# One stretch of row-group products in the output stage, and a later second spatial tile, in a fused attention and gMLP kernel

## The chip, the cores and the metric

The kernel runs on one core of a Trainium2 chip. The metric is device time in microseconds (us) for one execution; the median of several runs is compared. The core has five engines that matter here, each with its own in-order instruction stream: TensorE (PE in the profile; its weight loads are PEld), VectorE (DVE), ScalarE (ACT), GpSimd (POOL) and SyncE (SP). SP does no arithmetic; it issues transfers, as ACT and POOL can too. Transfers issued by one engine leave in the order of its stream. Sums of products land in PSUM, a small memory of banks with 512 float32 per partition each, and have to be read out before a bank is written for something else.

## The reference

Input x is [2048, 512] in bfloat16. The output is x plus two branches of the normalised x:

```python
xn = layernorm(x)                       # over the 512 features, eps 1e-5, no weights
# branch A: 32 heads of 16; each position attends to 8 earlier ones, 2 apart
q, k, v = xn @ wqkv                     # 512 -> 3 * 512
logits = (q[s] . k[s - 2 * w]) / 4      # w = 0..7, masked before position 0
a = softmax(logits over w) @ v[s - 2 * w] @ wo
# branch B: gated MLP with a mixing over positions
z = gelu(xn @ w_in)                     # 512 -> 2 * 688
z1, z2 = z[:, :688], layernorm(z[:, 688:])
g = w_sp @ z2 + b_sp[:, None]           # [2048, 2048] @ [2048, 688]
out = x + a + (z1 * g) @ w_out          # 688 -> 512
```

## The kernel before, in words

The 2048 positions are 16 tiles of 128 rows. The first third of the kernel normalises x, transposes it (`xnT`) and makes z2 (`z`, `h`), q and k (`k`) and z1 (`y`). ACT takes the gelu of each z2 tile and with it a row sum (`zsum`), then squares the tile to get a row sum of squares (`zsq`).

**Statistics of z2.** `z2_stats` (lines 246 to 252) runs once for four tiles (steps `zs0`, `zs4`, `zs8`, `zs12`): three small DVE operations make the mean and the variance, GpSimd adds EPS (line 251) and raises to the power -1/2 (line 252). Then DVE normalises the four tiles (`zn`, line 258). Between the two, DVE's list has larger work: the products of q with shifted k (line 307, steps `m` and `j`), whose folds (`f`, `p`, and transfers `d`) lead to the logits.

**The middle.** TensorE runs, in this order, the spatial tiles `M0` and `M1` (line 390: 32 products each, for 128 output positions), the head sums `S00` to `S13` (line 321, which turn the folded products into logits) mixed with eight `v` pairs (line 286), and then `M2` to `M15`. Each spatial tile fills one of three PSUM pairs, is emptied by ACT with its bias into one of three buffers (line 393), and is multiplied by z1 in a gate `g` on DVE (line 398). SP then transposes the gated rows by a transfer (line 400). The spatial weights come in eight pieces `W0` to `W7` (line 383), each for two spatial tiles, in three buffers; the buffer of `W3` is that of `W0`, so `W3` waits for `M1`.

**Softmax and attention on DVE.** For either half `th` of the positions: the maximum and its subtraction (`x`), an exponential on ACT (`e`), the sum (`u`), its inverse on ACT (`i`), the scaling (`c`), then twelve steps `a`: eight products of v with a weight (line 363), three additions (line 367), and a last addition (line 376) that writes the attention result for TensorE. All steps but the first of each half (w = 0) read v shifted by up to 14 rows, so they need the halo of v, two small transfers issued by GpSimd in `H` (lines 292 and 293), which in turn need all v copies of ACT.

**The output stage.** The 16 tiles form four groups of four (`groups`): two for the first half of the positions, two for the second. An output tile is the sum of five products with all 128 rows (`gated_full`, line 429), two with 32 and 16 rows for the remaining 48 gated features (`gated_rest`, line 444), and 16 with 32 rows for attention (`attention_out`, line 457). The products with 32 rows or fewer run for four tiles at once, each in its own group of 32 rows of the array ("row groups"). For the remainders, SP or GpSimd first copies rows to the right partitions (`spread_rest`, line 452). Eight banks hold two groups. `finish` and `finish_pair` add x (lines 462 and 469) and send the tile out.

**What sets the order.** Two lists are written by hand, `ten` (TensorE and ACT) and `vec` (DVE, with the transfers that belong to its steps). `advance` walks them: it takes steps in list order, and ahead of a step whatever `needs` names from the other list. The engines' streams follow that order. Waits between engines are added from what an instruction reads and writes.

Of the kernel before, what the change touches and what calls it, by code (L numbers as in the profile page):

```python
# [8 lines left out]
F32 = mybir.dt.float32  # L9
# [4 lines left out]
P = 128  # L14
# [24 lines left out]
def kernel(  # L39
# [36 lines left out]
    zmean = sb.tile([P, NT], F32, name="zmean")  # L76
    zvar = sb.tile([P, NT], F32, name="zvar")
    zrstd = sb.tile([P, NT], F32, name="zrstd")
    zbias = sb.tile([P, NT], F32, name="zbias")
    b16 = sb.tile([NT, P], BF16, name="b16")  # L80
    b_col = sb.tile([P, NT], F32, name="b_col")
    stmp = sb.tile([P, 4, GS], F32, name="stmp")
# [156 lines left out]

    def z2_square(i):  # L240

        A.activation(z2_junk[:], z2[:, i, :], ACT.Square, accum_out=zsq[:, i:i + 1])  # L242

    z2_junk = sb.tile([P, FH], BF16, name="z2_junk")

    def z2_stats(i, n):
        s = slice(i, i + n)
        V.tensor_scalar(zmean[:, s], zsum[:, s], 1.0 / FH, None, ALU.mult)
        V.tensor_tensor(zvar[:, s], zmean[:, s], zmean[:, s], ALU.mult)
        V.scalar_tensor_tensor(zvar[:, s], zsq[:, s], 1.0 / FH, zvar[:, s], ALU.mult, ALU.subtract)  # L250
        G.tensor_scalar(zvar[:, s], zvar[:, s], EPS, 1.0, ALU.add, ALU.mult)
        G.tensor_tensor(zrstd[:, s], zvar[:, s], mhalf[:, 0:n], ALU.pow)

    def z2_norm(i, on_act):
        if on_act:
            A.activation(z2[:, i, :], z2[:, i, :], ACT.Identity, bias=zbias[:, i:i + 1], scale=zrstd[:, i:i + 1])
        else:
            V.tensor_scalar(z2[:, i, :], z2[:, i, :], zmean[:, i:i + 1], zrstd[:, i:i + 1],
                            ALU.subtract, ALU.mult)

    def z1_tile(i):
        pz = z_part(i, 0)
# [176 lines left out]
    def gated_rest(tiles, start, last=None):  # L439
        for x in range(2):  # L440
            for i in tiles:
                rows, u, w = rest_of(i, x)
                for b, c in last if last and i == tiles[3] else [(po[i], slice(0, D))]:
                    PE.matmul(b[:, c], u, w[:, c], start=(start and x == 0), stop=False, tile_position=(rows.start, 0))  # L444

    def spread_rest(th, g):
        t = slice(2 * g * P, 2 * (g + 1) * P)
# [6 lines left out]
    def attention_out(th, s, pos, start, stop):  # L454
        for d in range(DH):
            for g in range(4):
                PE.matmul(pos[g], op[32 * g:32 * g + 32, th, d, s * P:(s + 1) * P], wo_r[32 * g:32 * g + 32, d, :],  # L457
                          start=(start and d == 0), stop=(stop and d == DH - 1), tile_position=(32 * g, 0))

    def finish(i, po, cols=slice(0, D), q=SP):  # L460
        o = nxt("ot", ot)
        V.tensor_tensor(o[:, cols], po[:, cols], xr[i // 8][:, i % 8, cols], ALU.add)  # L462
        q.dma_start(out2[i * P:(i + 1) * P, cols], o[:, cols])

    def finish_pair(i):

# [10 lines left out]
    for i in range(5, NT):  # L477
# [2 lines left out]
    vec = front.split() + """  # L480
        zs0 LW m00 zn0 zn1 zn2 zn3 j00 f00 p00 K m01 d01 m02 d02 zs4 m03 d03 zn4 zn5 zn6 zn7
        p01 p02 zs8 m10 d10 zn8 zn9 zn10 zn11 p03 W1 zs12 m11 zn12 zn13 zn14 zn15 f11 p11 p10 m12 d12
        m13 f13 x0 p13 p12 W2 W3 g0 u0 g1 c0 x1 a0.0 u1 g2
        c1 g3 a0.1 a0.2 a0.3 g4 a0.4 g5 a0.5 a0.6 a0.7 g6 a0.8 g7 a0.9 g8 a0.10 g9 a0.11 g10
        a1.0 a1.1 g11 a1.2 a1.3 g12 a1.4 g13 X1 a1.5 g14 a1.6 a1.7 g15 a1.8 a1.9 F0 a1.10 a1.11 F1 F2
    """.split()
    ten = """
        T0 B T1 GL BC z0 z1 h0 T3 h1 z2 h2 z3 h3 LZ k00 k01 q0 k02 q1 k03 q2 z4 h4 z5 q3 h5 k10 k12 k11 k13
        W0 q4 k20 z6 h6 q5 k21 z7 h7 q6 k22 z8 h8 q7 k23 z9 h9 q8 k30 z10 h10 q9 k31 z11 h11 q10
        k32 z12 h12 q11 k33 z13 h13 z14 h14 q12 z15 h15 y0 y1 q13 y2 y3 q14 y4 y5 q15 y6 y7 y8 y9 y10 y11 y12 y13 y14 y15  # L490
        EL M0 M1 S00 S01 v0 S02 S03 v1 S10 S11 v2 v3 e0 v4 v5 i0 v6 S13 S12 v7 H
        e1 M2 i1 M3 M4 O4 M5 W4 W5 M6 O0 M7 W6 M8 O1 M9 W7 M10 O2 M11 O3 M12 X0 M13 M14 M15 Q0 Q2 Q3
    """.split()

    def needs(n):
# [36 lines left out]
            return ["xeui"["euic".index(k)] + a]  # L532
        if k == "a":

            return ["c" + a[0]] + ([] if a == "0.0" else ["H"]) + ([f"y{x}" for x in range(NT)] if a[2:] == "11" else [])
        if k == "H":
            return [f"v{x}" for x in range(8)] + ["d12"]
        if k == "M":
# [9 lines left out]
        if k == "O":  # L548
            return [f"y{x}" for x in range(NT)] + ["H"]
        if k == "Q":  # L550
            return [["a0.11", "g7", "O4"], ["g7"], ["a1.11", "g15", "F0"], ["F2"]][i]
        if k == "F":
            return [f"Q{[0, 0, 2][i]}", f"X{i // 2}"]
        if k == "X":
            return ["M11" if i == 0 else "M13"]
        return []


    banks = [mm[1][:, 0, :], mm[1][:, 1, :], mm[2][:, 0, :], mm[2][:, 1, :],
             mm[0][:, 0, :], aux[0][:], mm[0][:, 1, :], aux[1][:]]  # L560
    groups = [[8 * th + 2 * g + t for g in range(4)] for th in range(2) for t in range(2)]
    po = {i: banks[4 * (n % 2) + g] for n, tiles in enumerate(groups) for g, i in enumerate(tiles)}

    def out_pair():

        first, second = groups[0], groups[1]
        for i in first:
            gated_full(i, po[i], True, False)
        gated_rest(first, False)
        gated_rest(second, True)  # L570
        attention_out(0, 0, [po[i] for i in first], False, True)
        attention_out(0, 1, [po[i] for i in second], False, False)
        for i in second:
            gated_full(i, po[i], False, True)

    def out_group(n):
        tiles = groups[n]
        for i in tiles:
            gated_full(i, po[i], True, False)
        gated_rest(tiles, False)  # L580
        attention_out(n // 2, n % 2, [po[i] for i in tiles], False, True)

    def out_last(n):

        tiles = groups[n]
        th, s, last = n // 2, n % 2, tiles[-1]
        hb = [po[last], po[groups[n - 1][0]]]
        cols = [slice(0, D // 2), slice(D // 2, D)]
        for d in range(DH):
            for g in range(4):  # L590
                a = slice(32 * g, 32 * g + 32)
                for dd, b, c in [(d, po[tiles[g]], slice(0, D))] if g < 3 else \
                        [(2 * d % DH + x, hb[d // 8], cols[d // 8]) for x in range(2)]:
                    PE.matmul(b[:, c], op[a, th, dd, s * P:(s + 1) * P], wo_r[a, dd, c],  # L594
                              start=(dd == 0), stop=False, tile_position=(32 * g, 0))
        gated_rest(tiles, False, list(zip(hb, cols)))
        for i in tiles[:3]:
            gated_full(i, po[i], False, True)
            finish(i, po[i])
        for b, c, q in zip(hb, cols, (SP, A)):  # L600
            gated_full(last, b, False, True, c)
            finish(last, b, c, q)

    gates, done = {}, set()
    at = [attend(0), attend(1)]
# [1 line left out]
    def do(n):  # L607
# [9 lines left out]
        elif n[:2] == "zs":  # L617
            z2_stats(int(n[2:]), 4)
        elif n[:2] == "zn":
            z2_norm(int(n[2:]), False)  # L620
        elif n == "z0":
            gates["z0"], gates["z1"] = nxt("mm", mm), nxt("mm", mm)
            for t, hh in ((0, 0), (0, 1), (1, 0)):
# [28 lines left out]
        elif k == "W":  # L652
            load_wsp(i)
        elif k == "O":
            load_wo(i) if i < 4 else load_wout()
        elif k == "X":
            load_res(i)
        elif n == "GL":
            A.preload_act_table(ACT.Gelu_apprx_tanh)
        elif n[:2] == "EG":  # L660
            A.preload_act_table(ACT.Gelu_apprx_tanh)
        elif n[:2] == "EL":
            A.preload_act_table_set("natural_log_exp_and_others")
        elif k == "Q":
            [out_pair, None, lambda: out_group(2), lambda: out_last(3)][i]()
        elif k == "F":
            tiles = groups[i]
            for t in (0, 2):
                if (i, t) in ((0, 0), (0, 2), (1, 0)):
                    finish_pair(tiles[t])  # L670
                else:
                    finish(tiles[t], po[tiles[t]])
                    finish(tiles[t + 1], po[tiles[t + 1]])
        elif k == "e":
            softmax_exp(i)
        elif k == "i":
            softmax_inv(i)
        elif k == "s":
            ln_stats(i)
        elif k == "R":  # L680
            ln_root_act(i, 1)
        elif k == "V":
            ln_inv(i)
        elif n == "LE":
            load_early()
        elif k == "r":
            ln_root(i, 1)
        elif k == "n":
            ln_norm(i)
        elif k == "t":  # L690
            turn_dma(i)
        elif n == "LZ":
            load_x(12, 4, A)
        elif n == "LX":
            load_tokens()
        elif n == "LW":
            load_weights()
        elif k == "m":
            run(prod_ops(th, w2)[0])
        elif k == "j":  # L700
            run(prod_ops(th, w2)[1])
        elif k == "f":
            prod_ops(th, w2)[2]()
        elif k == "p":
            prod_ops(th, w2)[3]()
        elif k == "d":
            fold_dma(th, w2)
        elif k == "K":
            k_halo()
        elif k == "x":  # L710
            run(softmax_max(i))
        elif k == "u":
            run(softmax_sum(i))
        elif k == "c":
            run(softmax_scale(i))
        elif k == "g":
            gate(i, gates[i])
            if i in (7, 9, 11, 13, 15):
                for g in range(4) if i == 7 else [(i - 9) // 2]:
                    spread_rest(i // 8, g)  # L720
        elif k == "a":
            at[int(a[0])][int(a[2:])]()
# [54 lines left out]
```

## Time and profile before

| what | us |
|---|---|
| median of 3 runs | 200.67 (200.47 to 200.71) |
| profiled execution, its own time | 200.75 |
| its span | 199.0 |
| TensorE busy | 194.4 |
| DVE busy | 176.0 |
| ACT busy | 89.2 |
| GpSimd busy | 46.7 |
| spatial products (line 390) | 75.0 |
| attention products and additions on DVE (lines 363 and 367) | 36.0 and 26.5 |

Times in the profile count from the start of the span. A timeline line has the start, the time, the engine, the line of the kernel, the operation and what it writes and reads; lines of the same kind that follow each other are merged (x4 is four of them), and a bracket gives the idle time of the engine ahead of the first and what ended it. TensorE's products overlap, so the time of one (0.38 for 512 columns) is longer than the distance of two (0.216).

The stages by TensorE's rows: z2, q, k and z1 until 72; `M0`, `M1` until 81.7; head sums and v pairs until 97.3; `M2` to `M15` until 162.7; the output stage until 196.1; then the last addition and transfer.

### The profile page before, as it was taken

What the parts mean: (1) busy time and instruction counts of PE and PEld (TensorE: products, weight loads), DVE (VectorE), ACT (ScalarE), POOL (GpSimd) and SP (SyncE); (2) the same over time, 40 slices, a digit from 0 to 9 for tenths busy, and PEclk for the clock granted to TensorE, in tenths of its full rate; (3) what the DMA queues carried; (4) which work ended last, traced back from release to release, by engine and by line L of the source; (5) the groups of instructions that cost most, each with busy time, mean ns of one, the idle gap of its engine ahead of it and who ended that gap; (6) DMA issues with size and microseconds to landing.
All of it is one profiled execution on the core that took longest, in us unless ns stands there. A gap on an engine that the chain in (4) does not pass through costs nothing.

```text
span 199.0 us, 3879 instructions
## 1 busy us (share of the span) xinstructions
PE 194.4 (98%) x1597; PEld 119.5 (60%) x1604; DVE 176.0 (88%) x193; ACT 89.2 (45%) x145; POOL 46.7 (23%) x71
## 2 busy tenths in 40 slices
PE   7999999999999999999999999999999999999993
PEld 2655555555666666666666666666666664444662
DVE  4899789999889899997898999999999999997233
ACT  3869779899888671489753111111222110000000
POOL 4277540139496701200060000101010000000000
PEclk9999999999999999999999999999999999999999
DMA  5999679399637961904999979999998934632033
GB/s 179 340 186 179 133 176 291 87 203 204 133 79 135 156 136 32 182 3 74 199 191 145 238 190 257 114 262 180 236 191 106 215 82 120 183 109 90 19 105 105
DMA packets 64610, 31.09 MB, mean 156 GB/s; under 512 B 53456, under 2 KB 62800, under 8 KB 64464
## 3 DMA queue, kind: packets, MB, share of 16 engines
q1 hardware_dynamic: 59136, 19.24, 48.5%
q0 software_dynamic: 2192, 6.75, 17.6%
q10 hardware_dynamic: 3264, 4.86, 10.4%
q8 instruction: 12, 0.20, 0.4%
q14 instruction: 6, 0.05, 0.1%
HBM read 10.13 MB, written 2.10 MB: 61 GB/s over the span
## 4 chain that ended last, share of the span: by engine, by line
PE 98%; issue 0%; DVE 0%
PE mm L390 38%; PE mm L226 19%; PE mm L271 14%; PE mm L286 7%; PE mm L429 7%; PE mm L457 5%; PE mm L405 2%; PE aux L429 2%; PE mm L594 1%; PE mm L444 1%; PE aux L321 1%; PE aux L212 1%; PE aux L594 0%; DVE z L462 0%; PE mm L645 0%
## 5 line engine op out<-in xcount | busy, mean ns | idle before, releaser
L390 PE MATMUL mm<-z,wsp 128*128 128x344 bf16 x512 | 75.0, 309 | 0.0
L390 PEld LDWEIGHTS <-wsp 128*128 128x128 bf16 x512 | 50.0, 98 | 24.9 <-issue 0.4
L226 PE MATMUL mm<-wts,xnT 128*128 128x344 bf16 x256 | 39.3, 309 | 0.1
L393 ACT ACTIVATE qk<-mm,b_col 128x688 bf16<-128x688 f32 x16 | 13.3, 833 | 52.6 <-PE mm L390 52.6
L363 DVE TENSOR_TENSOR prod<-vp,a_sb 128x4096 bf16<-128x4096 bf16 x16 | 36.0, 2281 | 0.0
L307 DVE TENSOR_TENSOR prod<-qk 128x4096 bf16<-128x4096 bf16 (+1 forms) x16 | 31.6, 2019 | 1.5 <-ACT qk L273 1.5
L226 PEld LDWEIGHTS <-xnT 128*128 128x128 bf16 x256 | 24.8, 98 | 13.3 <-DMA xnT<-z 0.3
L271 PE MATMUL mm<-xnT,wts 128*128 128x512 bf16 x124 | 28.7, 379 | 0.2
L367 DVE TENSOR_TENSOR prod<-prod,prod 128x8192 bf16<-128x8192 bf16 x6 | 26.5, 4418 | 0.1
L271 PEld LDWEIGHTS <-wts 128*128 128x128 bf16 x128 | 14.5, 114 | 12.2 <-DMA xnT<-z 0.4
L273 ACT CAST qk<-mm 128x1024 bf16<-128x1024 f32 x16 | 16.2, 1012 | 5.0 <-PE mm L271 4.1
L429 PE MATMUL mm<-wts,qk 128*128 128x512 bf16 (+1 forms) x62 | 14.2, 370 | 0.4 <-issue 0.3
L286 PE MATMUL mm<-xnT,wts 128*32 128x512 bf16 x256 | 14.5, 379 | 0.0
L263 ACT ACTIVATE z<-mm 128x688 bf16<-128x688 f32 x16 | 11.9, 742 | 4.4 <-PE mm L226 4.4
L429 PEld LDWEIGHTS <-qk 128*128 128x128 bf16 x85 | 8.2, 98 | 9.2 <-issue 0.6
L452 POOL DMA_DIRECT2D qk<-qk x6 | 3.0, 500 | 42.3 <-DMA qk<-z 42.3
L237 ACT ACTIVATE z<-mm 128x688 bf16<-128x688 f32 x16 | 11.9, 744 | 2.0 <-PE mm L226 1.9
L190 DVE BATCH_NORM_STATS2 stats<-z 128x6 f32<-128x512 bf16 x16 | 11.0, 685 | 1.8 <-DMA z<-in_A_x_dram 1.8
L316 POOL DMA_DIRECT2D prod<-prod x8 | 7.3, 994 | 22.3 <-DVE prod L307 22.3
L242 ACT ACTIVATE z_junk<-z 128x688 bf16<-128x688 bf16 x16 | 12.3, 772 | 0.0
L286 PEld LDWEIGHTS <-wts 128*32 128x32 bf16 x256 | 9.5, 138 | 4.3
L462 DVE TENSOR_TENSOR z<-mm,wsp 128x512 bf16<-128x512 f32 (+1 forms) x8 | 5.0, 651 | 7.8 <-PE mm L457 4.7
(98 smaller groups left out, 195.1 us busy)
## 6 DMA issues: line engine op xcount, KB each, us to landing
prod<-prod POOLq DMA_DIRECT2D x8, 512.0 KB, 5.2
wts<-in_A_wo_dram ACTq DMA_DIRECT2D x4, 512.0 KB, 5.6
out_dram<-z SPq DMA_DIRECT2D x9, 128.0 KB, 1.7
z<-in_A_x_dram SPq DMA_DIRECT2D x4, 256.0 KB, 4.3
wts<-in_A_wqkv_dram SPq DMA_DIRECT2D x2, 512.0 KB, 5.1
wsp<-wsp POOLq DMA_DIRECT2D x2, 512.0 KB, 5.7
wsp<-in_A_x_dram ACTq DMA_DIRECT2D x1, 1024.0 KB, 5.7
wsp<-in_A_x_dram SPq DMA_DIRECT2D x1, 1024.0 KB, 6.3
```

Source lines behind the costliest of these rows:

```text
L226: PE.matmul(pz[:, hh, 0:FHALF], xnT[:, kc, i * P:(i + 1) * P], w_z2[:, hh, kc] if part else w_z1[:, kc, hh * FHALF:(hh + 1) * FHALF], star ...
L237: A.activation(z2[:, i, :].rearrange("p (a b) -> p a b", a=2), pz[:, :, 0:FHALF], ACT.Gelu_apprx_tanh, accum_out=zsum[:, i:i + 1])
L242: A.activation(z2_junk[:], z2[:, i, :], ACT.Square, accum_out=zsq[:, i:i + 1])
L271: PE.matmul(pq[:, cc, :], w_c[:, kc], xnT[:, kc, t0:t0 + D], start=(kc == 0), stop=(kc == C - 1))
L273: A.copy(qk[b // 2][:, a, 2 * c2:2 * c2 + 2, o:o + D], pq[:])
L286: PE.matmul(pv[32 * g:32 * g + 32, dd, :], w, r, start=(kc == 0), stop=(kc == C - 1), tile_position=(0, 32 * g))
L307: ops.append(lambda ww=ww, k=k, c=c: V.tensor_tensor(pr[:, ww, c], q[:, c], k[:, c], ALU.mult))
L363: return lambda: V.tensor_tensor(dst, vp[:, :, th, off:off + GS], a_sb[:, th, w].unsqueeze(1).broadcast_to([P, DH, GS]), ALU.mult)
L367: return lambda: V.tensor_tensor(dst, dst, x, ALU.add)
L390: PE.matmul(pg[:, hh, 0:FHALF], w[:, k, (j % 2) * P:(j % 2 + 1) * P], z2[:, k, hh * FHALF:(hh + 1) * FHALF], start=(k == 0), stop=(k == NT ...
L393: A.activation(g.rearrange("p (a b) -> p a b", a=2), pg[:, :, 0:FHALF], ACT.Identity, bias=b_col[:, j:j + 1])
L429: PE.matmul(po[:, cols], uT[th][:, m, t0:t0 + P], wout[:, m, cols], start=(start and m == 0), stop=(stop and m == MF - 1))
```

## The change

It has four parts.

1. ACT's square of z2 is scaled by 688 to the power -1/2, so that its sum is already the mean of squares; the third DVE operation adds EPS and subtracts the squared mean; GpSimd is left with the power alone. (An unused variant of the normalisation goes too.)
2. `M1` moves on TensorE from behind `M0` to behind the last v pair and the halo `H`.
3. DVE's list is reordered from `W2` on: gates come later or earlier by a few steps, `W3` comes behind `g1`, the first attention step needs only the v pairs and no halo, and the first finished group (`F0`) moves behind the last attention step.
4. The output stage runs the whole products of both first groups, then the row-group products of all four groups, then the whole products of the last two groups. The remainders of group 2 wait for `F0`, which empties their banks. For the very last tile, DVE adds x to what its bank holds (`sofar`) ahead of its whole products; these then go in two column halves into two banks, and are added to `sofar`.

```diff
-        A.activation(z2_junk[:], z2[:, i, :], ACT.Square, accum_out=zsq[:, i:i + 1])
+        A.activation(z2_junk[:], z2[:, i, :], ACT.Square, scale=float(FH) ** -0.5, accum_out=zsq[:, i:i + 1])
...
-        V.scalar_tensor_tensor(zvar[:, s], zsq[:, s], 1.0 / FH, zvar[:, s], ALU.mult, ALU.subtract)
-        G.tensor_scalar(zvar[:, s], zvar[:, s], EPS, 1.0, ALU.add, ALU.mult)
+        V.scalar_tensor_tensor(zvar[:, s], zsq[:, s], EPS, zvar[:, s], ALU.add, ALU.subtract)
         G.tensor_tensor(zrstd[:, s], zvar[:, s], mhalf[:, 0:n], ALU.pow)
...
-        m13 f13 x0 p13 p12 W2 W3 g0 u0 g1 c0 x1 a0.0 u1 g2
-        c1 g3 a0.1 a0.2 a0.3 g4 a0.4 g5 a0.5 a0.6 a0.7 g6 a0.8 g7 a0.9 g8 a0.10 g9 a0.11 g10
-        a1.0 a1.1 g11 a1.2 a1.3 g12 a1.4 g13 X1 a1.5 g14 a1.6 a1.7 g15 a1.8 a1.9 F0 a1.10 a1.11 F1 F2
+        m13 f13 x0 p13 p12 W2 u0 g0 c0 x1 a0.0 u1 a0.1 g1 W3 c1 a0.2 g2 a0.3 g3
+        a0.4 g4 a0.5 g5 a0.6 a0.7 g6 a0.8 g7 a0.9 a0.10 g8 a0.11 g9
+        a1.0 a1.1 g10 a1.2 a1.3 g11 a1.4 g12 X1 a1.5 a1.6 g13 a1.7 g14 a1.8 g15 a1.9 a1.10 a1.11 F0 F1
...
-        EL M0 M1 S00 S01 v0 S02 S03 v1 S10 S11 v2 v3 e0 v4 v5 i0 v6 S13 S12 v7 H
-        e1 M2 i1 M3 M4 O4 M5 W4 W5 M6 O0 M7 W6 M8 O1 M9 W7 M10 O2 M11 O3 M12 X0 M13 M14 M15 Q0 Q2 Q3
+        EL M0 S00 S01 v0 S02 S03 v1 S10 S11 v2 v3 e0 v4 v5 i0 v6 S13 S12 v7 H
+        M1 e1 M2 i1 M3 M4 O4 M5 W4 W5 M6 O0 M7 W6 M8 O1 M9 W7 M10 O2 M11 O3 M12 X0 M13 M14 M15 Q0 Q2 Q3 Q4
...
-            return ["c" + a[0]] + ([] if a == "0.0" else ["H"]) + ([f"y{x}" for x in range(NT)] if a[2:] == "11" else [])
+            return ["c" + a[0]] + ([f"v{x}" for x in range(8)] if a == "0.0" else ["H"]) + ([f"y{x}" for x in range(NT)] if a[2:] == "11" else [])
...
-            return [["a0.11", "g7", "O4"], ["g7"], ["a1.11", "g15", "F0"], ["F2"]][i]
+            return [["a0.11", "g7", "O4"], [], ["a1.11", "g15", "F0"], ["F1"], ["Q3"]][i]
...
-    banks = [mm[1][:, 0, :], mm[1][:, 1, :], mm[2][:, 0, :], mm[2][:, 1, :],
+    banks = [mm[1][:, 0, :], mm[2][:, 0, :], mm[1][:, 1, :], mm[2][:, 1, :],
              mm[0][:, 0, :], aux[0][:], mm[0][:, 1, :], aux[1][:]]
...
+    def out_first():
+
+        for i in groups[0] + groups[1]:
             gated_full(i, po[i], True, False)
+        for n in (0, 1):
+            gated_rest(groups[n], False)
+        for n in (0, 1):
+            attention_out(0, n, groups[n], groups[n])
+
+    def out_tiled(n):
+        gated_rest(groups[n], True)
+        attention_out(1, n - 2, groups[n], [last])
+
+    def out_last():
+        V.tensor_tensor(sofar, po[last], xr[1][:, last % 8, :], ALU.add)
+        for i in groups[2] + groups[3][:3]:
             gated_full(i, po[i], False, True)
+            finish(i)
+
+        for b, c, q in ((po[last], slice(0, D // 2), SP), (po[groups[2][0]], slice(D // 2, D), A)):
+            gated_full(last, b, True, True, c)
+            o = nxt("ot", ot)
+            V.tensor_tensor(o[:, c], b[:, c], sofar[:, c], ALU.add)
+            q.dma_start(out2[last * P:(last + 1) * P, c], o[:, c])
```

More of the change, by code (lines that the diff above doesn't have):

```diff
@@ L78 @@
     zrstd = sb.tile([P, NT], F32, name="zrstd")
-    zbias = sb.tile([P, NT], F32, name="zbias")
     b16 = sb.tile([NT, P], BF16, name="b16")
@@ L249, in z2_stats, with z2_norm @@
         V.tensor_tensor(zvar[:, s], zmean[:, s], zmean[:, s], ALU.mult)
-        V.scalar_tensor_tensor(zvar[:, s], zsq[:, s], 1.0 / FH, zvar[:, s], ALU.mult, ALU.subtract)
-        G.tensor_scalar(zvar[:, s], zvar[:, s], EPS, 1.0, ALU.add, ALU.mult)
+        V.scalar_tensor_tensor(zvar[:, s], zsq[:, s], EPS, zvar[:, s], ALU.add, ALU.subtract)
         G.tensor_tensor(zrstd[:, s], zvar[:, s], mhalf[:, 0:n], ALU.pow)
[L254 to L259, printed above, removed]
+    def z2_norm(i):
+        V.tensor_scalar(z2[:, i, :], z2[:, i, :], zmean[:, i:i + 1], zrstd[:, i:i + 1], ALU.subtract, ALU.mult)
     def z1_tile(i):
@@ L437, in rest_of, with gated_rest @@
         return rows, uB[i // 8][rows, t0:t0 + P], wB[rows]
-    def gated_rest(tiles, start, last=None):
+    def gated_rest(tiles, start):
         for x in range(2):
@@ L442, in gated_rest @@
                 rows, u, w = rest_of(i, x)
-                for b, c in last if last and i == tiles[3] else [(po[i], slice(0, D))]:
-                    PE.matmul(b[:, c], u, w[:, c], start=(start and x == 0), stop=False, tile_position=(rows.start, 0))
+                PE.matmul(po[i], u, w, start=(start and x == 0), stop=False, tile_position=(rows.start, 0))
     def spread_rest(th, g):
@@ L452, in spread_rest, with attention_out, finish @@
                 (SP if th else G).dma_start(dst[32 * g:32 * g + n, t], uT[th][r:r + n, MF, t])
-    def attention_out(th, s, pos, start, stop):
+    def attention_out(th, s, tiles, stop):
         for d in range(DH):
             for g in range(4):
-                PE.matmul(pos[g], op[32 * g:32 * g + 32, th, d, s * P:(s + 1) * P], wo_r[32 * g:32 * g + 32, d, :],
-                          start=(start and d == 0), stop=(stop and d == DH - 1), tile_position=(32 * g, 0))
-    def finish(i, po, cols=slice(0, D), q=SP):
+                PE.matmul(po[tiles[g]], op[32 * g:32 * g + 32, th, d, s * P:(s + 1) * P], wo_r[32 * g:32 * g + 32, d, :],
+                          start=False, stop=(tiles[g] in stop and d == DH - 1), tile_position=(32 * g, 0))
+    def finish(i):
         o = nxt("ot", ot)
-        V.tensor_tensor(o[:, cols], po[:, cols], xr[i // 8][:, i % 8, cols], ALU.add)
-        q.dma_start(out2[i * P:(i + 1) * P, cols], o[:, cols])
+        V.tensor_tensor(o, po[i], xr[i // 8][:, i % 8, :], ALU.add)
+        SP.dma_start(out2[i * P:(i + 1) * P, :], o)
     def finish_pair(i):
@@ L550, in needs @@
         if k == "Q":
-            return [["a0.11", "g7", "O4"], ["g7"], ["a1.11", "g15", "F0"], ["F2"]][i]
+            return [["a0.11", "g7", "O4"], [], ["a1.11", "g15", "F0"], ["F1"], ["Q3"]][i]
         if k == "F":
-            return [f"Q{[0, 0, 2][i]}", f"X{i // 2}"]
+            return ["Q0", "X0"]
         if k == "X":
@@ L562 @@
     po = {i: banks[4 * (n % 2) + g] for n, tiles in enumerate(groups) for g, i in enumerate(tiles)}
-    def out_pair():
-        first, second = groups[0], groups[1]
-        for i in first:
+    last = groups[3][3]
+    sofar = wsp_r[1].bitcast(F32)[:, 0:D]
+    def out_first():
+        for i in groups[0] + groups[1]:
             gated_full(i, po[i], True, False)
[L569 to L573, printed above, removed]
-            gated_full(i, po[i], False, True)
@@ L576, in out_group @@
[L576 to L602, printed above, removed]
+        for n in (0, 1):
+            gated_rest(groups[n], False)
@@ L619, in do @@
         elif n[:2] == "zn":
-            z2_norm(int(n[2:]), False)
+            z2_norm(int(n[2:]))
         elif n == "z0":
@@ L664, in do @@
         elif k == "Q":
-            [out_pair, None, lambda: out_group(2), lambda: out_last(3)][i]()
+            [out_first, None, lambda: out_tiled(2), lambda: out_tiled(3), out_last][i]()
         elif k == "F":
-            tiles = groups[i]
             for t in (0, 2):
-                if (i, t) in ((0, 0), (0, 2), (1, 0)):
-                    finish_pair(tiles[t])
-                else:
-                    finish(tiles[t], po[tiles[t]])
-                    finish(tiles[t + 1], po[tiles[t + 1]])
+                if (i, t) == (1, 2):
+                    finish(groups[i][2])
+                    finish(groups[i][3])
+                else:
+                    finish_pair(groups[i][t])
         elif k == "e":
```

## The prediction

> **What bounds the kernel now.** I read the page first (busy shares, then the chain that ended last), then the list of waits, then the timeline around the three places that the change touches.
>
> ```profile
> PE 194.4 (98%) x1597; PEld 119.5 (60%) x1604; DVE 176.0 (88%) x193; ACT 89.2 (45%) x145; POOL 46.7 (23%) x71
> ...
> PE 98%; issue 0%; DVE 0%
> ```
>
> The reader is to see that TensorE is busy for 98% of the span and that the chain never leaves it. An edit therefore gains only if it takes work or gaps off TensorE, and loses exactly as much as it makes TensorE wait. DVE, with 88%, has the least room behind it. The profiled execution took 200.75 us (span 199.0), 0.08 above the median of the runs, 200.67; the sum below is made against 200.75 and 0.08 is taken off at the end.
>
> **Part 1, z2's statistics.** Of each of the four groups, the GpSimd addition of EPS (line 251) goes; EPS and the scale move into operations that are there already, at the same price. The timeline around the third group:
>
> ```profile
> 54.49 0.16 DVE L250 SCALAR_TENSOR_TENSOR zvar<-zsq,zvar 128x4 f32<-128x4 f32 x1
> 54.57 4.49 DVE L307 TENSOR_TENSOR prod<-qk 128x4096 bf16<-128x4096 bf16 x2
> 54.74 2.16 POOL L251 TENSOR_SCALAR zvar<-zvar 128x4 f32<-128x4 f32 x1 [2.68 <-DVE zvar L250]
> 56.99 2.96 POOL L252 TENSOR_TENSOR zrstd<-zvar,mhalf 128x4 f32<-128x4 f32 x1
> ...
> 59.99 0.46 DVE L258 TENSOR_SCALAR z<-z,zmean,zrstd 128x688 bf16<-128x688 bf16 x1 [0.94 <-POOL zrstd L252]
> ```
>
> While DVE runs its two products (4.49 us for both), the small GpSimd addition ends only at 56.90, where the first product ends (54.57 + 2.28 = 56.85); the power that follows ends 0.90 after the second one. Where DVE is idle (first group, at 24.4) the same two take 0.20 and 1.02. So a GpSimd operation is held up by a running DVE product, and the present pair needs two gaps. With one operation left, the power is in the place of the addition: it gets in at the first boundary (56.85) and is done about 1 us later, inside the second product. DVE's wait of 0.94 then goes in the groups at 44, 54 and 63 us. Bounds: nothing, if the power makes the second product wait instead (rival A); 0.94 each. I take 0.94, because the addition got through the boundary without lengthening either product: the two take 4.49 with it, and 4.49 also at 35.50, where GpSimd runs no arithmetic. The third wait is limited from elsewhere: line 250 of the fourth group needs ACT's last square, done at 62.19, so it can move from 63.19 only to 62.25. DVE is earlier by 0.94 + 0.94 = 1.84 us there (0.94 up to line 250, 0.9 after it); call this lead G = 1.8. Alone it gives TensorE nothing: the first mixing product starts at 72.3, the last row group of z2 was ready at 70.24.
>
> **Part 2, the second spatial tile behind the v pairs.** TensorE's amount of work stays. M1 is 32 products of 0.146 = 4.66 us, so all of the v stage starts 4.66 earlier (77.0 instead of 81.66), and M2 starts where it did, 97.31. What was hidden behind M1 must now be ready 4.66 earlier.
>
> ```profile
> 90.10 1.22 DVE L311 TENSOR_TENSOR wts<-prod 128x2048 bf16<-128x2048 bf16 x1
> ...
> 95.19 0.39 PE L321 MATMUL aux<-wts,rsel 128*32 128x512 bf16 x4
> 95.41 1.90 PE L286 MATMUL mm<-xnT,wts 128*32 128x512 bf16 x32
> ```
>
> The last head sum S12 starts at 95.19 and needs the fold that ends on DVE at 91.32. It would start at 90.53, so G must be over 0.85; with 1.8 there is 0.95 to spare. The pair behind it, v7, would start at 90.75. It reuses the PSUM pair of v4, whose copy on ACT stands behind the first exponential, which waits for DVE's line 335 (end 89.05): 89.05 - G + 0.06 + 1.91 (exponential) + 1.0 (copy) = 92.0 - G. G must be over 1.3, and there is 0.5 to spare. Cost 0, with this cover named.
>
> Then DVE's list, durations from the rows of before: the last fold ends at 89.5; the sum of the exponentials (2.41) at 92.0; g0 0.43; the scaling c0 2.25, behind ACT's 0.95 for the inverse; the second maximum (2.65) ends at 97.9. ACT meanwhile copies v6, two head sums, v7 (end 95.9), at 97.31 to 98.18 it empties M1, then runs the second exponential until 100.1, while DVE runs a0.0. The second sum ends at 102.55, and a0.1 could start there. It now also waits for the halo of v: its two GpSimd transfers are issued after v7's copy, 96.2 and 97.7. Before they landed 8.3 and 7.4 us after issue, beside two spatial-weight loads; the fastest transfer on that queue takes 3.9. That gives 101.6 to 105.1. I take 102.6 as the start of a0.1, since only the first of those two loads now lies near it. (Before: 109.25, but with g1, g2, g3 and c1 already done.)
>
> **W3**, the load for M6 and M7, moves behind g1 in DVE's list and, in SP's queue, from right behind W2 to behind the transposes of g0 and g1. So it is issued 2.2 (a0.1) + 0.45 (g1) + 1.3 (SP's issue of g1's transpose) + 0.15 = 4.1 after the start of a0.1: at 106.7 instead of 95.83. TensorE needs it at 97.31 + 4 x 4.66 = 115.97.
>
> ```profile
> wsp<-in_B_w_sp_dram SPq DMA_TRANSPOSE x8, 9.2
> ```
>
> ```profile
> DMA to landing us min/median/max: 6.2/9.2/10.4
> ```
>
> The eight of these land 6.2 to 10.4 us after issue. The slow ones stood behind row-group transposes or another load; the ones near an empty queue took 7.9 (at 91.4), 6.2 (116.1) and 7.4 (135.1). I take 7.5 and get 114.2, 1.8 in time; with the median 115.9, just in time; with 10.4 late by 1.1. W4 behind it goes out near 113, lands by 123, and is needed at 125.3. Cost 0, up to 1.1 (to 3.6 with the latest halo). The other gates keep their distance: by the durations every g comes at least 2.5 us after its mixing tile is emptied and 4 us before its buffer is needed.
>
> **Part 3, the output stage.** The products are as many (85 of 128 rows counting halves, 32 of four row groups each for the remainders, 256 instead of 272 for attention, where the 32 halves cost what 16 whole ones do). Moved are only the changes between whole and row-group products: two ways there and back become one.
>
> ```profile
> 174.88 8.32 PEld L429 LDWEIGHTS <-qk 128*128 128x128 bf16 x40 [0.42 <-issue]
> 175.11 1.03 PE L429 MATMUL mm<-wts,qk 128*128 128x512 bf16 x4 [0.16 <-issue]
> ...
> 178.39 2.29 DVE L376 TENSOR_TENSOR xnT<-prod 128x4096 bf16<-128x4096 bf16 x1
> ...
> 183.62 0.12 PEld L444 LDWEIGHTS <-qk 32*128 32x128 bf16 x8 [0.42 <-issue]
> ```
>
> Within either kind a step takes 0.216. The last whole product before 183.63 begins at 183.32 (the row at 183.10 has two), so that way costs 183.63 - 183.32 - 0.216 = 0.1. Back, the last attention step begins at 174.57 and the first weights load at 174.88: 0.1. (The first tile shows x4 of its five products, so a record is missing; taken at face value 175.11 would make it 0.3.) One way there and back is 0.2, at most 0.4. This is the only sure gain: -0.2.
>
> What it risks is order. Before, 40 whole products (8.6 us) lay between the th=0 attention and the th=1 attention and covered DVE's last operation, which ends at 180.68. After, TensorE starts the stage at 162.6, needs 40 x 0.216 + 0.1 + 0.88 + 6.91 = 16.5 and wants group 2's remainders at 179.1. These need F0's four additions (2.4 us) to have emptied the first four banks, and attention needs a1.11. DVE from the start of a0.1 to the end of a1.11 took 71.43 (109.25 to 180.68); now g1, g2, g3 (1.3) and c1 (2.2) are inside and F0 (2.4) is behind: 72.5. So a1.11 ends at 175.1, F0 can start when the first attention half ends, 175.8, and ends at 178.3: in time by 0.8, as long as a0.1 starts before 104.4. F1 (2.4 from 179.3) is wanted at 183.0. The remainders of the last rows (SP: g15's transpose at 167.5, its spread 5.3 later, 2.5 to land, so about 177) are in time by 2. The load X1, on SP ahead of g13's transpose, waits for M13 at 158.0 and holds nothing up. M15's emptying (end 163.62) is wanted at 163.8 now that the second bank is the one that it leaves. After the last product the end is as before: half an addition (0.42) and a transfer. The extra addition for the last tile (0.69) lies beside 7.5 us of products.
>
> **Sum:** 200.75 - 0.2 = 200.55, less 0.08: **200.45 us**.
>
> **Rivals.** A, slower: the port decides. The power, let in at the boundary, keeps the second product out until it is done, 0.9; then G is 0. S12 waits 0.87 and v7 in all 92.05 - 90.75 = 1.3; a0.1 starts near 104.5, which W3 and F0 still bear because TensorE is later too. 200.75 - 0.2 + 1.3 - 0.08 = 201.8. It decides below G = 1.3. For it: the power at 56.99 waits for the whole product, so something exclusive is there. Against it: a one-column power at 22.77 (0.55) and a DVE operation at 22.71 (0.41) overlap, and neither is longer than its neighbours.
>
> ```profile
> 22.71 0.41 DVE L207 TENSOR_SCALAR z<-z,mv,rstd 128x512 bf16<-128x512 bf16 x1 [0.31 <-POOL rstd L197]
> 22.77 0.55 POOL L198 TENSOR_TENSOR rstd<-rstd,mhalf 128x1 f32<-128x1 f32 x1
> ```
>
> The Trainium skill ("SBUF — State Buffer", section "SBUF: two separate sides") says of the port pair that DVE and GpSimd share that whichever starts first has it for its whole instruction and that the other fully blocks; by that rule the time would be A's 201.8, while the sum by the rows is 200.45. The overlap at 22.77 does not look like that rule, the wait at 56.99 does.
>
> B, slower: W3 is late. It takes a landing of 9.3 or more, or a halo later than 104.4. With 10.4 the time is 200.45 + 1.1 = 201.55; with a halo at 105.1 and 9.2 it is 200.45 + 2.4 = 202.85. For it: the old landings under load. Against it: fewer transfers in flight at 107.
>
> C: DVE is late at the output stage (F0 past 179.1) for a reason that I don't see; each us of it costs one, about 201.2. Against it: every step of DVE's list comes from a row.
>
> D, faster: the way there and back is worth its face value of 0.4 or more: 200.2 or less.
>
> E: no change that can be told, which the forecast amounts to, since 0.2 of 200.67 is 0.1%; about 0.2% is what a measurement of this kernel can tell from none.
>
> **How the numbers follow.** The forecast (nothing late, -0.2) has 0.52, A 0.16, B 0.13, C 0.07, D 0.12. D alone is faster by over 0.2%: 0.12. A, B and nearly all of C are slower by over 0.2%: 0.35. The rest, 0.53, is within. The forecast's own range is 200.2 to 200.7. The range for 8 in 10 reaches from D's 200.15 to A's 201.8 and leaves out B's far end.
>
> **What would show it.** Right: no wait of DVE's line for z2's normalisation on GpSimd; two products there still 4.49; TensorE without a gap from 77 to 116 and from 179 to 196; stage changes two fewer. Wrong: the second product at 56.8 lasting 3 us or a gap of TensorE ahead of S12 or v7 (A); a gap ahead of M6 with W3's landing at its end (B); one ahead of the th=1 remainders (C).

## The result, and the profile after

The changed kernel is slower: the ratio of its time to that of the kernel before is 1.0045, 95% interval 1.0031 to 1.0059. Its four executions that count took 201.34, 201.63, 201.71 and 201.72 us, against a median of 200.69 before, so +0.9 us. Executions more than 1.5% longer than the fastest of the same kernel are left out of every comparison here, among them four of this kernel's eight (208.9 to 209.8 us) and five of e6's six, and what makes them long is not shown.

The profiled execution took 201.34 us with a span of 199.6 (before: 200.75 and 199.0), so the trace has +0.6 us to explain; the other three executions are 0.3 longer still and have no profile. From the page of the changed kernel, the busy shares and the chain that ended last:

```profile
PE 194.4 (97%) x1580; PEld 117.9 (59%) x1586; DVE 176.9 (89%) x194; ACT 89.2 (45%) x145; POOL 40.1 (20%) x67
...
PE 89%; DMA 6%; DVE 3%; issue 1%; POOL 0%
```

TensorE's busy time has not moved, but the chain now leaves it: 6% of the span is DMA. The chain in order of time (start, time, what) says which transfer:

```profile
92.67 13.97 PE mm L384 x96
106.65 9.96 DMA wsp<-in_B_w_sp_dram
116.61 0.14 issue
116.74 8.33 PE mm L384 x56
```

The spatial tiles M1 to M3 run from 92.67, and then the chain jumps to `W3`, which SP issues at 106.65 and which lands 9.96 later. M6 starts at 116.74. The timeline around it:

```profile
106.65 5.54 SPq L377 DMA_TRANSPOSE wsp<-in_B_w_sp_dram  x1
...
111.55 0.37 ACTq L406 DMA_DIRECT2D wts<-in_B_w_out_dram  x1
...
116.71 0.56 PEld L384 LDWEIGHTS <-wsp 128*128 128x128 bf16 x5 [0.95 <-issue]
116.74 0.74 PE L384 MATMUL mm<-z,wsp 128*128 128x344 bf16 x4 [0.62 <-DMA wsp<-in_B_w_sp_dram]
```

The first product of M6 begins 0.93 after the last one of M5, where 0.15 is the normal step: a gap of 0.79. The line in the middle is a second load (`O4`, the output weights: 640 KB here, then four small transfers) that ACT sends out while the packets of `W3` are on their way.

The other places that the change touches look like this. Statistics of z2, third group:

```profile
53.51 0.16 DVE L249 SCALAR_TENSOR_TENSOR zvar<-zsq,zvar 128x4 f32<-128x4 f32 x1
53.59 4.49 DVE L301 TENSOR_TENSOR prod<-qk 128x4096 bf16<-128x4096 bf16 x2
53.76 3.02 POOL L250 TENSOR_TENSOR zrstd<-zvar,mhalf 128x4 f32<-128x4 f32 x1 [3.19 <-DVE zvar L249]
...
58.00 0.45 DVE L253 TENSOR_SCALAR z<-z,zmean,zrstd 128x688 bf16<-128x688 bf16 x1
```

The power ends at 56.78 (53.76 + 3.02), 0.91 after the boundary between the two products (55.87) and inside the second one. Both still take 4.49, and DVE's normalisation has no bracket: its wait is gone, as are the three waits of line 258 on line 252 in DVE's list of waits. At the last head sum and the last v pair:

```profile
88.16 1.22 DVE L305 TENSOR_TENSOR wts<-prod 128x2048 bf16<-128x2048 bf16 x1
...
90.56 0.39 PE L315 MATMUL aux<-wts,rsel 128*32 128x512 bf16 x4
90.78 0.60 PE L280 MATMUL mm<-xnT,wts 128*32 128x512 bf16 x7
```

The fold ends at 89.38 (91.32 before, 1.94 earlier), and neither S12 nor v7 has a bracket, so neither waits. At the output stage:

```profile
176.68 2.48 DVE L462 TENSOR_TENSOR z<-mm,wsp 128x512 bf16<-128x512 f32 x4 [1.48 <-PE mm L450]
...
179.93 0.37 PE L437 MATMUL mm<-wts,qk 32*128 32x512 bf16 x1
```

`F0` empties the four banks by 179.16; TensorE wants them at 179.93 and does not wait. From the first whole product to the end of the last one the stage takes 33.22 us (163.40 to 196.63); before it took 33.48 (162.59 to 196.06).

So the trace adds up: +0.79 (M6) - 0.26 (stage) + 0.03 (everything up to M5) = +0.56, against +0.6 in the spans. A term as small as the last one says nothing: the first spatial product starts at 72.16 before and at 72.19 here, and in the traces of the experiments anywhere from 71.91 to 72.57, with the same TensorE work ahead of it.

### The profile page after: what moved, and what is told of

It is laid out like the page before. It is cut to its first block, busy times and chain, and to the rows that moved or that the text cites. A ratio compares the mean times of both kernels' runs of the same rounds, so it can differ in the third digit from the quotient of the medians.

```text
span 199.6 us, 3847 instructions
## 1 busy us (share of the span) xinstructions
PE 194.4 (97%) x1580; PEld 117.9 (59%) x1586; DVE 176.9 (89%) x194; ACT 89.2 (45%) x145; POOL 40.1 (20%) x67
## 4 chain that ended last, share of the span: by engine, by line
PE 89%; DMA 6%; DVE 3%; issue 1%; POOL 0%
PE mm L384 33%; PE mm L225 18%; PE mm L265 14%; PE mm L280 7%; PE mm L450 7%; PE mm L423 7%; DMA wsp<-in_B_w_sp_dram 5%; PE aux L423 2%; DVE stats L189 1%; DMA z<-in_A_x_dram 1%; PE aux L315 1%; PE mm L437 1%; DVE z L206 1%; DVE mv L190 0%; POOL rstd L197 0%
## 5 line engine op out<-in xcount | busy, mean ns | idle before, releaser
L450 PE MATMUL mm<-wts,xnT 32*128 32x512 bf16 x192 | 14.3, 374 | 0.0
```

The lines of the kernel that those rows point to most:

```text
L450: PE.matmul(po[tiles[g]], op[32 * g:32 * g + 32, th, d, s * P:(s + 1) * P], wo_r[32 * g:32 * g + 32, d, :], start=False, stop=(tiles[g] in ...
```

## The experiments

After the result the theory was: the loss is `W3`, late because it is issued behind a0.1 and g1 and lands in 10.0 instead of 7.5; everything else is as predicted. The rivals: the output stage or one of the moved gates costs something of its own. The kernels change the lists of steps (`vec`, `ten`) or undo a part; all but one give a comparison of times.

**e1: `W3` earlier.**

```diff
-... c0 x1 a0.0 u1 a0.1 g1 W3 c1 a0.2 g2 a0.3 g3
+... c0 x1 a0.0 u1 W3 a0.1 g1 c1 a0.2 g2 a0.3 g3
```

> The changed kernel with W3 one place earlier on DVE's list (ahead of a0.1 and g1, so right behind the second sum of exponentials), nothing else. Theory (the late W3 is the whole loss): W3 is issued near 102.6 instead of 106.65, lands by 112.5, M6 starts 0.146 after the last product of M5 instead of 0.93, and the time falls by 0.8 from the changed kernel, to 200.4 to 200.6, 0.1% below the kernel before. Rival (M6's gap is only a part, or stands for something else such as the new order of the gates or of the output stage): the time stays over 201.1.

Measured: ratio to before 1.0001 (0.9991 to 1.0011), about 200.6 us, 1.0 under the changed kernel; profiled 200.84, span 199.1. `W3` goes out at 102.47, lands at 110.6, and M6 follows M5 by 0.146: the gap is gone. But the output stage now takes 33.66, 0.44 more than in the changed kernel, so that the two profiled executions differ by only 0.5 (201.34 and 200.84). The timeline of TensorE's weight loads there:

```profile
179.18 0.10 PEld L437 LDWEIGHTS <-qk 32*128 32x128 bf16 x4 [0.34 <-DMA qk<-qk]
...
179.61 0.09 PEld L437 LDWEIGHTS <-qk 16*128 16x128 bf16 x1 [0.32 <-DMA qk<-qk]
```

The remainders, wanted from 178.95 on, wait for the spread rows of g15 (0.7 us over two waits). SP's stream shows where those became late:

```profile
160.57 1.28 SPq L394 DMA_TRANSPOSE qk<-z  x1
161.94 0.54 SPq L416 DMA_DIRECT2D wsp<-in_A_x_dram  x1
162.57 1.32 SPq L394 DMA_TRANSPOSE qk<-z  x1
```

The load `X1` (line 416, 1 MB) leaves between the transposes of g12 and g13; the one behind it lands 8.2 us after issue, the one ahead of it 2.8. g14 and g15 queue behind, and the last spread rows land at 179.56. In the changed kernel the same load stands in the same place, but there the transpose behind it lands 6.2 after issue, and SP sends the spread of g15 out in time:

```profile
174.66 1.15 SPq L445 DMA_DIRECT2D qk<-qk  x2
```

Those rows land at 176.96, almost 3 us before they are wanted at 179.93. So `X1` costs the changed kernel nothing; why the transpose behind it took 2 us longer in e1 is not shown. Theory on `W3` holds; a second delay stood behind it.

**e2: `W3` later,** behind g2 in `vec`.

```diff
-... u1 a0.1 g1 W3 c1 a0.2 g2 a0.3 g3
+... u1 a0.1 g1 c1 a0.2 g2 W3 a0.3 g3
```

> The changed kernel with W3 behind g2 instead of behind g1. Theory (W3 decides): by the rows of the changed kernel g2 ends at 110.0 and its transpose leaves SP at 111.2, so W3 is issued near 111.3 and lands 8 to 10 us later; M6, wanted at 115.95, waits 3.4 to 5.4 us, and the time is 204 to 206.3. Rival (the gap ahead of M6 has another cause): the time stays at 201.6 within 0.5.

Measured: 216.29 us, ratio 1.078 (1.0765 to 1.0794), far more than expected. M6 again starts when `W3` lands, from the chain in order of time:

```profile
123.04 6.43 DMA wsp<-in_B_w_sp_dram
129.61 49.09 PE mm L384 x320
```

What the expectation had wrong is the place: the walk of the lists took M5, W4 and W5 before it came to this step, so on SP `W3` is the third of three loads (111.78, 118.58, 123.04). The gap ahead of M6 is 13.4. That explains 12.5 of the 14.7 over the changed kernel (13.43 against 0.93 from product to product; 216.3 against 201.6); most of the rest lies in the granted clock of TensorE behind the gap, from the view by stretches (stretch, its length, PE busy with the number of products, the other engines, granted clock, DMA):

```profile
130.00:135.00 5.00, 5.00 (x22) 2.66 (x20) 0.00 (x0) 0.00 (x0) 0.51 (x1) 0.58 0.22 43
135.00:140.00 5.00, 5.00 (x36) 3.35 (x35) 2.40 (x2) 0.83 (x1) 0.00 (x0) 1.00 0.45 105
```

In the first 5 us TensorE gets through 22 products at a mean clock of 0.58, in the next 5 us 36 at 1.00: 14 fewer at 0.146 each are 2.0 us.

The direction and the place of the wait are those of the theory; the size of one step of the list was misjudged.

**e6: `O4` behind M6,** all else as changed, to ask why `W3` lands in 10.0.

```diff
-... M3 M4 O4 M5 W4 W5 M6 O0 M7 ...
+... M3 M4 M5 W4 W5 M6 O4 O0 M7 ...
```

> The changed kernel with the load O4 (the output weights, issued by ACT at 111.6 while W3 is under way) moved behind M6 on TensorE's and ACT's list. Theory (W3 landed in 10.0 instead of 7.5 us because O4 shares the transfer engines with it): W3 lands about 8 us after issue, 114.7, M6 has no gap, 200.4 to 200.6. Rival (W3's landing is long by itself or behind the transpose of g1): W3 still takes about 10 us and the time stays at 201.3 to 201.7.

No comparison of times came of it (one execution that counts, 201.22, which is neither the 200.4 to 200.6 of the theory nor the 201.3 and more of the rival). The trace is of an execution of 210.9 us; up to 130 us its granted clock is 1.00, as in the changed kernel, and only that part is read. In it `W3` is issued at 106.58, within 0.1 of the changed kernel, and line 377 there says

```profile
DMA to landing us min/median/max: 7.8/7.8/7.8
```

where the same answer for the changed kernel says

```profile
DMA to landing us min/median/max: 10.0/10.0/10.0
```

M6 does not wait. With `O4` out of the way the load lands in 7.8, near the 7.5 of the forecast, although the transpose of g1 stands ahead of it and that of g2 and `W4` behind it, as in the changed kernel. That is one landing of each kind, but three other traces agree: where `W3` has landed before `O4` goes out it takes 8.1 (e1), 7.8 (e11) and 7.6 (e9). So `O4` beside it is the best account of the 2.2. What moving `O4` does to the time stays open.

**e4: the new output stage alone** on the kernel before (statistics, place of M1 and order of gates as before; the lines of the stage itself as in the change, left out here).

```diff
-... a1.8 a1.9 F0 a1.10 a1.11 F1 F2
+... a1.8 a1.9 a1.10 a1.11 F0 F1
-... M15 Q0 Q2 Q3
+... M15 Q0 Q2 Q3 Q4
```

> The kernel before with the new output stage alone (F0 and F1 behind a1.11, banks as in the changed kernel; statistics, order of M1, W3 and gates as before). Theory: the stage saves 0.25 us of mode changes, but the cover is gone: a1.11 ends at 178.3, F0's additions at 180.7, and TensorE wants the emptied banks at 179.1, so it waits 1.6; 200.7 - 0.25 + 1.6 = 202.0. Rival (the second group's banks or F0 do not hold the row-group products up): 200.45.

Measured: 202.67, ratio 1.0094 (1.0081 to 1.0107). TensorE's list of waits and DVE's timeline in that trace:

```profile
PE mm L438 <- DVE z L463: 1.3, 2, 1.0
```

```profile
176.25 2.29 DVE L371 TENSOR_TENSOR xnT<-prod 128x4096 bf16<-128x4096 bf16 x1
...
178.46 3.08 DVE L463 TENSOR_TENSOR z<-mm,wsp 128x512 bf16<-128x512 f32 x5
```

```profile
181.32 0.58 PE L438 MATMUL mm<-wB,qk 16*128 16x512 bf16 x2
```

DVE's last attention step ends at 178.54 and `F0` only starts then. Its four additions empty the banks one after another, 0.6 apart, so the four tiles are let in one by one: the last remainder (the second of the last line) starts at 181.52, where a stage without waits that begins at 162.66 has it at 179.41 (16.75 in, as in e11). These 2.11 are the whole loss: 33.22 + 2.11 is the 35.33 that the stage takes. The expectation counted 1.6 of it, up to the last addition, and so came out 0.5 low. Without the earlier DVE that the rest of the change gives, the new stage loses more than its one saved change between whole and row-group products.

**e5: the statistics alone** on the kernel before.

```diff
-A.activation(..., ACT.Square, accum_out=...)
+A.activation(..., ACT.Square, scale=float(FH) ** -0.5, accum_out=...)
...
-G.tensor_scalar(zvar[:, s], zvar[:, s], EPS, 1.0, ALU.add, ALU.mult)
```

> The kernel before with the statistics of z2 changed alone. Theory (DVE gains 1.9 us up to the second half of its products, TensorE never waited there): DVE's waits for GpSimd vanish, the time stays within 0.2 of the kernel before. Rival (an earlier DVE brings the later stages forward, too): 0.4 or more below the kernel before.

Measured: 1.0003 (0.9994 to 1.0012). DVE's waits go, the time stays: part 1 alone gives TensorE nothing.

**e7: `W3` still earlier,** behind x1, meant to keep clear of `O4` altogether.

```diff
-... c0 x1 a0.0 u1 a0.1 g1 W3 c1 ...
+... c0 x1 W3 a0.0 u1 a0.1 g1 c1 ...
```

> The changed kernel with W3 right behind the second maximum on DVE's list, the first place at which M1 has freed its buffer. Theory (the only loss is the late W3, and the loads behind it on SP were pushed back with it): W3 is issued near 97.6 and lands by 106, W4 to W7 go out within 1 us of their times in the kernel before (107.5, 116.1, 125.4, 135.1), M6 to M15 have no gap, and the time is 200.4, the forecast for the whole change, 0.1% below the kernel before. The halo now shares the transfers with W3: a0.1 may start up to 2 us later than 102.5, which costs nothing up to 104.4. Rival (the new order costs something apart from W3): 200.9 or more.

Measured: 1.0054 (1.0037 to 1.0071), no better than the changed kernel. The expectation was wrong. `W3` lands at 106.8 and M6 does not wait, but DVE's timeline shows what it now collides with:

```profile
104.44 2.29 DVE L357 TENSOR_TENSOR prod<-vp,a_sb 128x4096 bf16<-128x4096 bf16 x1 [2.16 <-DMA vp<-vp]
```

The halo of v lands 8.9 and 7.9 us after issue instead of 5.3 and 4.1, a0.1 starts at 104.44 instead of 102.48, and all of DVE's list is late by that: `F0` ends at 179.5, the remainders wait for it and for the spread of g15, and the stage takes 34.16 (+0.94). `W4` to `W7` were expected within 1 us of before and go out 3 to 6 later (113.4, 119.1, 131.1, 140.3), but no spatial tile waits for them.

**e8: e7 with the output stage of before.** It asks whether e7's loss is in the new stage.

```diff
-... M15 Q0 Q2 Q3 Q4
+... M15 Q0 Q2 Q3
-... a1.8 g15 a1.9 a1.10 a1.11 F0 F1
+... a1.8 g15 a1.9 F0 a1.10 a1.11 F1 F2
```

> The kernel before with the statistics, M1's place and DVE's list of the run with W3 behind x1, but with its own output stage (F0 between a1.9 and a1.10). Theory (parts 1 and 2 give TensorE nothing, the output stage alone gives 0.25): 200.65, the kernel before within 0.1, and 0.25 above the run with W3 behind x1; from the first whole product of the stage to its last 33.48 us against 33.22. Rival (part of a gain comes from the middle): below 200.5.

Measured: 0.9999 (0.999 to 1.0008), stage 33.48 as before, as expected: the old stage has 40 whole products in front of the same remainders and hides it when DVE is late. It is a milder case than e7, though: here the halo landed in 7.9 and 7.1, and a0.1 starts at 103.62, 1.1 later than in the changed kernel instead of 2.0.

**e3: e7 with both GpSimd operations back,** to measure what part 1 is worth with part 2.

```diff
-V.scalar_tensor_tensor(zvar[:, s], zsq[:, s], EPS, zvar[:, s], ALU.add, ALU.subtract)
+V.scalar_tensor_tensor(zvar[:, s], zsq[:, s], 1.0 / FH, zvar[:, s], ALU.mult, ALU.subtract)
+G.tensor_scalar(zvar[:, s], zvar[:, s], EPS, 1.0, ALU.add, ALU.mult)
```

> The run with W3 behind x1, with the two GpSimd operations for the root of z2's variance put back. Theory (DVE's lead of 1.9 us is what covers the head sum S12 and the pair v7, which come 4.66 us earlier): the 0.94 us waits of DVE return three times, S12 starts 0.85 us late and v7 in all 1.25 us late, and the time is 201.6 to 201.7, 1.25 above the run with W3 behind x1. Rival (the lead is not needed): 200.4.

Measured: 1.0088 (1.0064 to 1.0111), 0.7 us over e7 by the ratios, whose intervals overlap (1.25 was expected); its profiled execution is the longest of four, and its span, 201.6, is 2.05 over e7's, 0.47 of it ahead of the first spatial product. DVE's waits are back, and TensorE's timeline has two new ones:

```profile
91.59 0.40 PE L316 MATMUL aux<-wts,rsel 128*32 128x512 bf16 x4 [0.68 <-DVE wsp L377]
...
92.23 1.09 PE L281 MATMUL mm<-xnT,wts 128*32 128x512 bf16 x16 [0.23 <-ACT vp L283]
```

Counted from the first spatial product, S12 starts 19.22 us in, where e7 and the changed kernel have 18.37, and v7 at 19.85 for 18.58: 0.85 and in all 1.27 late, just what was expected (the forecast had 0.87 growing to 1.3 for a lead of zero). So part 2 needs part 1: by the trace, not by a clear difference of the times.

**e11: e1 with `X1` behind g15,** to test the second delay by taking it away.

```diff
-... a1.4 g12 X1 a1.5 a1.6 g13 a1.7 g14 a1.8 g15 a1.9 ...
+... a1.4 g12 a1.5 a1.6 g13 a1.7 g14 a1.8 g15 X1 a1.9 ...
```

> The run with W3 before g1, with the load X1 (1 MB of x, on SP) moved from ahead of g13's transpose to behind g15's. Theory (the 0.43 us that this run's row-group stretch lost is TensorE waiting for the copy of g15's last rows, which is late because g13's transpose landed 8.2 us after issue behind X1 and held SP's stream): g13's transpose lands in about 3, the copies go out 4 us earlier, the waits ahead of the remainders vanish, the stretch from first to last whole product is 33.2 instead of 33.66, and the time is 200.1 to 200.3. Rival (F0's additions hold the remainders): the stretch stays at 33.6 and the time at 200.5.

Measured: 200.35 us (200.24 to 200.61 over 11 executions), ratio 0.9988 (0.9979 to 0.9997), span 198.6. SP's stream:

```profile
159.15 0.52 SPq L445 DMA_DIRECT2D qk<-qk  x1
159.72 2.61 SPq L394 DMA_TRANSPOSE qk<-z  x2
```

The transposes leave without `X1` between them and land in 2.8; the remainders do not wait, TensorE has no gap at M6 or in the stage, and the stage takes 33.22. With both late transfers put right, the kernel comes out 0.25 us faster than the one before (200.1 to 200.3 was expected): a gain of 0.1%, which the interval just tells from none, and as much as the stage saves.

**e9: e11 with g2 and its transpose early,** to see whether `W4` to `W7` come sooner for it.

```diff
-... u1 W3 a0.1 g1 c1 a0.2 g2 a0.3 g3
+... u1 W3 g1 g2 a0.1 c1 a0.2 a0.3 g3
```

> The same, and g1 and g2 both ahead of a0.1 (list: u1 W3 g1 g2 a0.1 c1 a0.2 a0.3 g3). Theory (in the changed kernel g2's transpose stands ahead of W4 on SP, g2 comes 4 us later than before, and so W4 to W7 go out 2 to 6 us later and meet other loads): W4 is issued near 109.6 instead of 113.6, W5 near 116.1, W7 near 135.5 and lands by 145 as in the kernel before; no gap in M2 to M15, none in the output stage, and 200.1 to 200.4. Rival (W4 to W7 depend on the other loads, not on g2): W7 still lands at 147 or later, and the time is that of the run with X1 behind g15.

Measured: 0.9992 (0.9984 to 1.0001), span 198.8, not better than e11. `W4` is issued earlier (110.45) but takes 12.1 to land; `W7` lands at 146.3 (147.4 in the changed kernel). The theory that g2's place delays the loads fell: `W7` lands when it does in e11 (146.2), although that is a little before the 147 of the rival. That the landings depend on what else is moving, `O4` among it, fits all of this but is not tested by itself here.

## Why the prediction was right or wrong

**Wrong: the landing of `W3`.** The step that failed reads "the ones near an empty queue took 7.9 ..., 6.2 ... and 7.4 ... I take 7.5 and get 114.2, 1.8 in time". It measured 10.0, and 116.6 was 0.65 too late. The issue was right to 0.1 (106.7 forecast, 106.65 measured), the time of need too (115.97; M5's last product and one step give 115.95), so in the trace the whole miss is this one term. Its reason, given against rival B as "fewer transfers in flight at 107", was false: the prediction nowhere counts ACT's `O4`, issued from 111.5 on in both kernels. e6 has the landing without it, 7.8, and so do e1, e11 and e9, where `W3` has landed before `O4` goes out (8.1, 7.8, 7.6). The forecast's own sorting would have put `W3` among the long landings, too, since it leaves right behind the row-group transpose of g1; but in e6 it does so as well and lands in 7.8. The nearest row of before was that of `W4`, issued at 107.45 and also beside `O4` (line 383, at 107.45):

```profile
DMA to landing us min/median/max: 9.2/9.2/9.2
```

With it the forecast's sum gives 115.9, just in time and 0.1 short of rival B's point of decision. So the right row would have taken away the 1.8 to spare, but not shown the wait; no row explains the 0.8 between 9.2 and 10.0.

**Rival B is what happened,** with a gap of 0.79 for 1.1 at a landing of 10.4. That its 201.55 is so close to the 201.6 of the ratio is partly luck: the profiled execution has +0.6, and the further 0.3 of the other executions is unexplained.

**Right: part 1.** The power gets in at the boundary and is done 0.91 later, the second product is not lengthened, the lead is 1.94 for 1.8 forecast. That excludes rival A. By the rule quoted with it from the Trainium skill ("SBUF — State Buffer", section "SBUF: two separate sides"), the second product would have been shut out until the power ended; the trace does not agree, with 4.49 for the two products as before, and the measurement decides. The other half of the rule, that GpSimd waits for a DVE product that came first, is as the trace has it: 3.02 for a power that takes 1.02 where DVE is idle. That the lead is worth nothing alone is e5's 1.0003.

**Right: S12, v7 and the halo.** Neither waits; the lead has to exceed 0.85 and 1.3, and e3, which takes it away, has the waits that rival A priced (1.27 for 1.3). a0.1 starts at 102.48 (102.6 forecast). The bound at the other end, a halo beside a spatial load, is e7: 104.44.

**Right: the output stage,** -0.26 for -0.2, and `F0` in time by 0.77 for 0.8. The limit of 104.4 for a0.1 was too generous: e7, with a0.1 at 104.44, loses 0.94 in the stage, part of it to the late spread of g15, which the limit left out. Rivals C and D did not come: nothing there is late in the changed kernel, and the way there and back is not worth 0.4.

**Wrong in its reason, at no cost here: "The load X1 ... holds nothing up".** The forecast let `X1` go from 158 on; it left at 162.29 in the changed kernel, behind g12's transpose, and g13's transpose behind it landed in 6.2 instead of 2.8. Even so the remainders of the last rows land at 176.96, as forecast (about 177), and are in time by almost 3 (2.1 without the gap ahead of M6; the forecast had 2). In e1 three things come together: g13's transpose lands in 8.2, the spread of g15 takes 2.7 to 2.9 instead of 1.7, and TensorE is 1 us earlier; there the rows are late. e11 takes both late transfers away and measures 200.35, where the forecast had 200.45: the sum fits a kernel in which these two loads do not get in the way, which is not the kernel that was forecast.

## What to carry to other kernels

Take a transfer's landing from the row that has the same neighbours at the same time, on every queue, not from the row with the emptiest queue: here the load next door, beside the same ACT transfer, showed 9.2 where 7.5 was assumed and 10.0 came, so leave room beyond that row as well. Where a late transfer is put right, look at once for the next one: moving a load changes what stands beside the others. Each load that stands in a queue ahead of small, urgent transfers is a candidate. Parts that measure as nothing or a loss alone (statistics 1.0003, output stage 1.0094) can still be what another part stands on.

## What was not expected of the hardware

Landings differed with what else was moving far more than the forecast allowed: the same 1 MB load landed in 10.0 beside `O4` and in 7.8 without it (e6); the halo in 5.3 and 4.1, or 8.9 and 7.9 beside `W3` (e7); a row transpose in 2.8, or 6.2 (changed kernel) and 8.2 (e1) behind `X1`. The long wait of TensorE in e2 cost more than itself: after the gap of 13.4 us the granted clock was 0.58 over the next 5 us, and the kernel lost some 2 us there beyond the gap; around the 0.79 gap of the changed kernel the clock is 1.00 throughout.
